# Six column pieces of W1 behind the first keys, and a key product over two heads of both batches, in a planned DeltaNet and MLP kernel

## Chip, cores and metric

One core of one Trainium2 chip runs the whole program. The metric is the device time of one execution in microseconds (us); lower is better. The kernel before was timed three times: median 530.33, lowest 530.28, highest 531.17.

## What is computed

Four batches, 8 heads, 768 positions, head size 48, all float32. First a delta-rule recurrence for each batch and head, then a normalised two-layer MLP with a residual over the 384 joined head outputs:

```
k_n = k / (norm(k, axis=-1) + 1e-6)
for t in range(S):
    y[t]  = q[t] @ state
    v_old = k_n[t] @ state
    state = state + beta[t] * outer(k_n[t], v[t] - v_old)
x  = y with its heads joined              # (4, 768, 384)
xn = (x - mean) / sqrt(var + 1e-6) * g_ln
out = x + relu(xn @ w_ch1) @ w_ch2        # 384 -> 1536 -> 384
```

## The kernel before

**Chunks.** The 768 positions are cut into 12 chunks of 64 (`C`), and a chunk into two blocks of 32 (`BK`). All 32 pairs of batch and head go through a chunk together: four groups of 8 heads by partition half and position in the row (`hp`, `e`, `g`). Inside a chunk the recurrence becomes matmuls: the products of keys with keys and of keys with queries, the inverse of a triangular matrix for each block, a correction step (`u`), the output (`y`) and the update of the state (`s_all`).

**Engines.** TensorE turns keys and queries (`first_kt`, L840, for early chunks) and does all products. The stages of `recur` are: keys times state (L1216 into `two`), corrections in three products (L1256: diagonal block, below, diagonal block), queries times state (L1216 into `by`), state update (L1281) and output (L1271). ScalarE copies a correction result out of PSUM at L1266 and the output of a chunk at L1312. VectorE subtracts at L1221 and L1262.

**The inverses.** Chunks 0 and 1 use `gram_near`, a 16-row elimination on VectorE (`rows_near`, L1088 and L1095) and a join of the two halves on TensorE (`near_join`, L1140). Later chunks take a 32-row elimination for two chunks at once (`rows_inverse`: L1157, 31 pairs of L1178 and L1185, and L1190, which writes the result). Its diagonal blocks come from copies on ScalarE: for chunks 2 and 3 L907 (with L911 for the block below the diagonal), behind the product `gram` (L896); from chunk 4 on L1030 and L1042.

**The merged key product.** From chunk 4 on `gram_queries` makes the key-key and key-query products of a chunk in one go, in two halves (`gram_half`, matmuls at L1017): half `g` writes the PSUM pair `two` (`g` = 0) or `by` (`g` = 1) for batch parity `g` and all four head pairs `j`. A matmul has 48 rows and 32 columns of stationary data and sits on one of eight tiles of the array. Where the block `b` equals `g` it streams 128 columns (`w` = `C`, two segments), otherwise 64 (`w` = `BK`). After it ScalarE copies the diagonal blocks (L1030, three copies of 128 elements per half) and the off-diagonal ones (L1042, two copies of 256), and VectorE masks the query product into `pt` (L1035).

**The MLP.** A chunk gives 256 rows. Chunks 0 to 2 run the first layer directly (L1561: twelve feature tiles `f0` to `f11`, three matmuls each, one for each 128 rows of W1), later chunks in a form with fewer products (`eleven`, L1492). The second layer is L1583 for chunk 0 and `seven` (L1664) afterwards, with combinations of weights and activations made on GpSimd and VectorE.

**Weights.** W1 and W2 arrive as 64-bit words on ScalarE's DMA queue, in 12 pieces of 768 KB (`fetch`), and are made into float32 by `convert`: two steps on ScalarE (L798, L806), one on VectorE (L803) and one on GpSimd (L816). A piece of W1 is 128 rows by 768 columns, 6 KB in one run per row, so the first feature tiles need three pieces. The three pieces with the first 768 columns are converted in two halves of 384 columns.

**Order.** The order of the instructions is worked out when the kernel is built. `Line.add` records each step with its engine, an assumed cost, what it reads and writes, and for MLP products a due time. `Line.schedule` places the steps by priority, and `emit` issues them in that order; every engine then works strictly in its own order. The lists `DUE`, `CAP`, `T0` and `OFF` shift due times, limits, earliest starts and priorities. `PASS`, `UPER` and the numbers in `pe(...)` are the costs that the planner assumes for short matmuls. `after=` in a step orders the plan alone; on the chip an instruction waits only for data that it reads or overwrites. Matmuls at L1745 keep TensorE busy in the first part and give nothing to the result.

**DMA queues.** SP issues keys, queries, values, most of beta and the outputs. ScalarE issues half of chunk 0's keys and all pieces of W1 and W2. GpSimd issues eight small loads of beta and the norm weights.

Of the kernel before, what the change touches and what calls it, by code (L numbers as in the profile page):

```python
# [56 lines left out]
def act(n):  # L57
    return 0.17 + 0.83e-3 * n
# [371 lines left out]
def kernel(  # L430
# [34 lines left out]
    UPER = 0.0076  # L465
# [57 lines left out]
    pmask = sb("pmask", [128, 2, C])  # L523
# [4 lines left out]
    lane = sb("lane", [128, 6])  # L528
    beta_s = sb("beta_s", [128, NEAR, FB])
# [24 lines left out]
    DUE = [-305.067857599, -184.157488926, 455.196580585, 43.3608971536, 325.931658715, 418.81557092, 734.822875439, 596.087521503, 954.313194593, 1226.15149798, 1753.77174886, 1187.43924725, -1.6924469742, 7.47712706956, 1.31274637377, 1177.34078649]  # L554
    CAP = [747.889715428, 1212.19696458, 1084.81830387, 1850.25080892, 1448.91733639, 908.561376039, 705.970562755, 575.226842462, 821.351411096, 750.46942201, 1687.9172189, 1227.4281115, 847.781737921, 881.489018474, 1102.45793961, 1447.53022967, 1091.57755388]
    T0 = [32.9830988769, 43.9377940451, 29.0921020937, 44.9281472705, 63.7206388166, 107.721780452, 109.01717894, 42.4201425188, 137.327678312, 9.9371017997, 7.55135349446, 21.1072922972, 47.3695615515, 3.2653345546, 12.003557196, 58.3820362978, 9.11313409582, 34.3183793157, 80.7294725245, 31.0940483985, 65.2240956281, 73.1210354066, 26.5270080195, 53.6799046277, 66.9289646085, 120.165225966]
# [39 lines left out]
    def dma(eng, out_, in_, n, ns, r=(), w=(), **kw):  # L596

        cost = 0.65 if eng == "Pool" else 0.39 if ns == 300 else 0.68 if ns in (16.5, 16) else 0.46 if ns == 168 else 0.62 if n < 128 else 0.53
        add(eng, cost, lambda: QUEUE[eng].dma_start(out=out_, in_=in_), r, w, bulk=n * ns / 16e3, pk=ns, **kw)  # L599
# [64 lines left out]
    for e in range(2):  # L664
        c_pool(
            lambda e=e: nc.gpsimd.affine_select(
                out=pmask[half(e), 0], in_=pmask[half(e), 0], compare_op=ALU.is_gt, fill=0.0, base=0,
                pattern=[[1, C]], channel_multiplier=-1,
            ),
            0.3, ["pmask"],  # L670
        )
    for x in range(4):
        c_pool(
            lambda x=x: nc.gpsimd.affine_select(
                out=pmask[quad(x), 1], in_=pmask[quad(x), 1], compare_op=ALU.is_gt, fill=0.0, base=BK * (x % 2 - 1),
                pattern=[[1, C]], channel_multiplier=-1,
            ),
            0.3, ["pmask1"], r=["pmask"],
        )
# [71 lines left out]

    def tb_keys(i, kind):

        if kind == "blk":
            return [("blk", i, hp, m, u) for hp in range(2) for m in range(2) for u in range(2)]
        return tb_nat(i, (kind,))

    def tb_nat(i, kinds=(0, 1)):
        return [("tb", i, e, g, *o) for g in kinds for e in range(2) for o in ((), (0,), (1,), (2,))] + [("tbpad", i)]


    pieces = [
        (w1_sb[:, t, f : f + WN], w_ch1.bitcast(U32)[t * 128 : (t + 1) * 128, 2 * f : 2 * (f + WN)], ("w1", t, f // WN))
        for f in range(0, DFF, WN)
        for t in range(KC)
    ] + [
        (
            w2_sb[:, t : t + 2],
            w_ch2.bitcast(U32)[t * 128 : (t + 2) * 128].rearrange("(t p) n -> p t n", p=128),
            ("w2", t // 2),  # L770
        )
        for t in range(0, FT, 2)
    ]
    BUF = [3, 4, 0, 1, 2, 5, 6, 0, 1, 2, 0, 1]

# [3 lines left out]
    def fetch(i, **kw):  # L779
        line.part += 1  # L780
        dst = words[BUF[i]].rearrange("p n w -> p (n w)")
        src = pieces[i][1]
        if len(src.shape) == 3:
            dst = dst.rearrange("p (t n) -> p t n", t=2)
        dma("ACT", dst, src, 128, 300, w=WORD_KEYS[BUF[i]], after=raw_keys(0) if i < 2 else (), **kw)

    def convert(i, c0=0, n=WN, **kw):
# [19 lines left out]
        if len(dst.shape) == 3:  # L807
            f0 = c0 // DM
            dst, keys = dst[:, f0 : f0 + n // DM], [key + (f0 + x, y) for x in range(n // DM) for y in range(2)]
            shape = lambda x: x.rearrange("p (t n) -> p t n", n=DM)  # L810
        else:
            dst, keys = dst[:, cols], [key + (c0 // 384 + x,) for x in range(n // 384)]
            shape = lambda x: x
# [183 lines left out]
    def gram_half(c, g, ps, pk, **kw):  # L997
# [5 lines left out]

        def segs(ap, step, n):
            return bass.AP(tensor=ap.tensor, offset=ap.offset, ap=[ap.ap[0], [step, 2], [1, n]])

        def prod():
            for j in range(NP):
                for hp, e in hp_e:
                    lk, lq = (((2 * x + g) * NP + j) * C for x in (key_half(c, hp, e), e))  # L1010
                    for b in range(2):
                        o = ps[quad(2 * (e ^ hp) + b), hp, j * 2 * C : (j + 1) * 2 * C]
                        if b == g:
# [878 lines left out]
```

## Time and profile before

| | us |
|---|---|
| median of 3 runs | 530.33 |
| the profiled execution | 531.07 |
| its span | 529.2 |
| TensorE matmul busy | 501.5 |
| VectorE busy | 369.4 |
| GpSimd busy | 211.3 |
| ScalarE busy | 196.7 |
| TensorE idle from 100 to 500 us | 5.0 |

The profile is of one execution. The time of that execution is 1.9 us longer than its span, which runs from the first to the last event that the profiler saw. A line of a timeline gives the start, the length, the engine, the source line and the operation; in brackets stands the idle time before it and what ended it. In the names of engines PE is TensorE's matmul, PEld its weight load, DVE VectorE, ACT ScalarE, POOL GpSimd and SP SyncE; a "q" behind a name is its instruction queue. A matmul of the source is two instructions in the trace, because float32 goes through in two passes, so a stage of 32 matmuls shows as x64. Where a trace misses records, a stage shows fewer.

### The profile page before, as it was taken

Reading aid. Unit: us, or ns where it says so; the run is one execution under the profiler, and the core shown is the slowest. Engines: PE = TensorE matmul, PEld = TensorE weight load, DVE = VectorE, ACT = ScalarE, POOL = GpSimd, SP = SyncE. Lnnn points to the kernel's source line nnn. Section 1 sums busy time; section 2 is a strip of 40 time slices with the busy share of each in tenths; the row PEclk is TensorE's granted clock in tenths of the full one; section 3 lists DMA queues with packets and bytes.
Section 4 is the critical chain, followed back from the end, with each engine's and each line's share of the span. In section 5 each row is a group of like instructions: output and inputs, shape, how many; then the busy total and the mean of one; then the engine's idle time right before and its main releaser. Section 6 shows DMA issues by size and latency. Waiting matters only on the chain.

```text
span 529.2 us, 22198 instructions
## 1 busy us (share of the span) xinstructions
PE 501.5 (95%) x9706; PEld 455.5 (86%) x9706; DVE 369.4 (70%) x849; ACT 196.7 (37%) x420; POOL 211.3 (40%) x320
## 2 busy tenths in 40 slices
PE   5967799999999999999999989999999999999996
PEld 3746677768898999989999879999889999999995
DVE  1899559997399866889895589895688893452331
ACT  2834875513812623525204522513523213242030
POOL 6151422236333560642724242452351815235352
PEclk8576779999999999999999999999999999999999
DMA  9965544365645445455311435221233010221101
GB/s 156 281 140 122 86 129 130 94 93 86 86 67 84 90 81 81 94 75 115 59 31 19 67 86 92 51 61 33 58 70 91 1 30 5 63 62 29 31 2 30
DMA packets 157457, 40.53 MB, mean 77 GB/s; under 512 B 150816, under 2 KB 153888, under 8 KB 157360
## 3 DMA queue, kind: packets, MB, share of 16 engines
q1 hardware_dynamic: 153520, 29.40, 31.4%
q10 hardware_dynamic: 3552, 9.63, 5.7%
q8 instruction: 76, 1.25, 1.0%
q0 software_dynamic: 288, 0.07, 0.1%
q14 instruction: 21, 0.17, 0.1%
HBM read 30.82 MB, written 8.26 MB: 74 GB/s over the span
## 4 chain that ended last, share of the span: by engine, by line
PE 86%; DVE 6%; issue 2%; DMA 2%; ACT 2%; SPq 1%; POOL 0%; DVEq 0%; ACTq 0%
PE f L1664 28%; PE f L1492 25%; PE f L1561 10%; PE two L1256 4%; PE f L1583 3%; PE by L1216 2%; PE two L1216 2%; PE by L1271 2%; PE two L1281 2%; PE two L1017 2%; DMA kr<-in_k_dram 1%; PE f L1140 1%; SPq L599 1%; DVE tmp L1088 1%; PE by L1017 1%
## 5 line engine op out<-in xcount | busy, mean ns | idle before, releaser
L1650 POOL TENSOR_TENSOR h_all<-h_all 128x256 f32<-128x256 f32 x99 | 73.9, 751 | 79.1 <-PE f L1664 65.9
L1664 PE MATMUL f<-w_sb,h_all 128*128 128x192 f32 x396 | 97.1, 333 | 1.4 <-ACT xln L1336 0.8
L1664 PE MATMUL f<-words,h_all 128*128 128x192 f32 x396 | 90.1, 329 | 0.0
L1492 PE MATMUL f<-xnt,w_sb 128*128 128x128 f32 x648 | 87.1, 277 | 0.4 <-issue 0.4
L1492 PEld LDWEIGHTS f<-xnt,w_sb 128*128 128x128 f32 x648 | 80.0, 192 | 1.6 <-ACT xnt L1377 0.9
L1664 PEld LDWEIGHTS f<-w_sb,h_all 128*128 128x128 f32 x396 | 66.3, 190 | 5.1 <-issue 2.3
L1515 DVE TENSOR_TENSOR h_all<-f,h_all 128x512 f32<-128x512 f32 (+1 forms) x90 | 49.5, 555 | 28.9 <-PE f L1492 19.8
L1664 PEld LDWEIGHTS f<-words,h_all 128*128 128x128 f32 x396 | 67.6, 190 | 1.1 <-ACT xln L1336 0.2
L1689 POOL TENSOR_TENSOR words<-h_all 128x128 f32<-128x128 f32 x66 | 32.8, 515 | 86.0 <-ACT h_all L1512 76.4
L1185 DVE TENSOR_TENSOR xb<-xb,tmp 128x31 f32<-128x31 f32 (+15 forms) x155 | 61.3, 396 | 4.0
L1178 DVE TENSOR_TENSOR tmp<-xb,gb 128x31 f32<-128x31 f32 (+15 forms) x155 | 60.0, 387 | 5.2 <-POOL xb L1164 1.0
L1561 PE MATMUL f<-xnt,w_sb 128*128 128x256 f32 x216 | 54.6, 399 | 1.2 <-issue 1.2
L1561 PEld LDWEIGHTS f<-xnt,w_sb 128*128 128x128 f32 x216 | 41.5, 198 | 8.2 <-issue 1.7
L1266 ACT COPY u<-two 128x768 f32<-128x768 f32 x24 | 19.2, 800 | 51.3 <-PE two L1256 43.8
L1492 PE MATMUL f<-second,w_sb 128*128 128x128 f32 x216 | 33.1, 276 | 1.7 <-POOL second L1472 1.7
L1512 ACT ACTIVATE h_all<-f 128x512 f32<-128x512 f32 (+1 forms) x36 | 17.4, 489 | 42.7 <-PE f L1492 31.0
L1682 DVE TENSOR_TENSOR o<-f,x 128x192 f32<-128x192 f32 x33 | 11.6, 352 | 30.5 <-PE f L1664 22.7
L1664 PE MATMUL f<-w_sb,words 128*128 128x192 f32 x132 | 32.1, 328 | 0.0
L1570 ACT ACTIVATE h_all<-f 128x256 f32<-128x256 f32 x36 | 13.7, 384 | 49.2 <-PE f L1561 49.0
L1492 PEld LDWEIGHTS f<-second,w_sb 128*128 128x128 f32 x216 | 29.2, 192 | 2.0 <-POOL second L1472 2.0
L1512 ACT ACTIVATE h_all<-h_all 128x512 f32<-128x512 f32 (+1 forms) x36 | 18.7, 521 | 29.4 <-DVE h_all L1515 29.3
L856 POOL TENSOR_TENSOR v<-v,knrms 128x768 f32<-128x768 f32 x10 | 15.3, 1533 | 30.4 <-PE f L1561 11.4
(194 smaller groups left out, 858.6 us busy)
## 6 DMA issues: line engine op xcount, KB each, us to landing
words<-in_moe_w_ch_dram ACTq DMA_DIRECT2D x8, 768.0 KB
out_dram<-o SPq DMA_DIRECT2D x48, 96.0 KB
xld<-xlt SPq DMA_DIRECT2D x9, 384.0 KB
xnt<-xld SPq DMA_DIRECT2D x36, 96.0 KB
tb<-in_q_dram SPq DMA_DIRECT2D x40, 64.0 KB
tb<-in_k_dram SPq DMA_DIRECT2D x32, 64.0 KB
v<-in_v_dram SPq DMA_DIRECT2D x8, 192.0 KB
w_sb<-in_moe_w_ch_dram ACTq DMA_DIRECT2D x2, 768.0 KB
```

Of the source, the lines that this page charges most:

```text
L1178: lambda j=j, n=n, w=w, t=t: nc.vector.tensor_tensor(out=t, in0=xb[:, 0:n, j : j + 1].to_broadcast([128, n, w]), in1=gb[:, j : j + 1, j + ...
L1185: "DVE", dve(n * w), lambda t=t, rest=rest: nc.vector.tensor_tensor(out=rest, in0=rest, in1=t, op=ALU.subtract),
L1216: nc.tensor.matmul(dst[half(e), hp, j], src[drows(hp), (e if n else key_half(c, hp, e)) * GP + j], s_all[drows(hp), e, j], start=(n == 0 o ...
L1256: nc.tensor.matmul(*args(e, e ^ hp, 2 * j + hp))
L1266: add("ACT", act(768), lambda: nc.scalar.copy(u_j, p_2), TWO, uk, after=["nought", *SMALL] if not c else (), **kw)
L1492: nc.tensor.matmul(wide(p[:, o : o + 128]), w[:, f : f + 128], r, start=start and m == n == 0, stop=stop, skip_group_check=True)
L1512: add("ACT", act(128 * m), lambda: nc.scalar.activation(to[0], p, ACTF.Relu), pk, to[1])
L1515: add("DVE", dve(128 * m), lambda v=ps(p): nc.vector.tensor_tensor(out=to[0], in0=v, in1=y[0], op=op), [*pk, *y[1]], to[1])
L1561: nc.tensor.matmul(p[:, 0:TOK], w1_sb[:, t, f * 128 : (f + 1) * 128], xnt[:, t], start=(t == 0), stop=(t == KC - 1))
L1650: add(eng, cost, lambda: e.tensor_tensor(out=out_, in0=x, in1=y, op=op), r, w, port=2 if eng == "Pool" else 1, pr=-2)
L1664: lambda f=f, t=start and f == 0: nc.tensor.matmul(p[:, 0:D2], lhs(f), rhs[:, f], start=t, stop=(f == F2 - 1), skip_group_check=True),
L1689: lambda f=f + i: e.tensor_tensor(out=s3[f], in0=one(0, 0)[0](f), in1=one(1, 0)[0](f), op=ALU.subtract),
```

## The change

The pieces of W1 are cut by columns: six pieces of 256 columns with all 384 rows, in runs of 2 KB. A piece carries two feature tiles. A small ScalarE copy that reads chunk 0's raw keys stands ahead of all fetches, and each piece is converted whole. The merged key product takes in each half two of the four head pairs, of both batch parities. The masks (`pmask`) and the copies behind the product follow, and the off-diagonal copy becomes four copies of 128 elements per half. The planner's costs for two kinds of short matmuls are changed, and the four lists have new numbers, so that all instructions are ordered anew. The numbers of the lists are left out here.

```diff
-    UPER = 0.0076
+    UPER = 0.0102
+    GPER = 0.0125
...
-    pmask = sb("pmask", [128, 2, C])
+    pmask = sb("pmask", [128, NP, C])
...
+    seen = sb("seen", [128, 2])
...
     pieces = [
-        (w1_sb[:, t, f : f + WN], w_ch1.bitcast(U32)[t * 128 : (t + 1) * 128, 2 * f : 2 * (f + WN)], ("w1", t, f // WN))
-        for f in range(0, DFF, WN)
-        for t in range(KC)
+        (
+            w1_sb[:, :, f : f + WN // KC], w_ch1.bitcast(U32)[:, 2 * f : 2 * (f + WN // KC)].rearrange("(t p) n -> p t n", p=128),
+            ("w1", f * KC // WN),
+        )
+        for f in range(0, DFF, WN // KC)
     ] + [
...
-        dma("ACT", dst, src, 128, 300, w=WORD_KEYS[BUF[i]], after=raw_keys(0) if i < 2 else (), **kw)
+        dma("ACT", dst, src, 128 * src.shape[1], 300 / src.shape[1], w=WORD_KEYS[BUF[i]], after=["seen"], **kw)
...
+        HP = NP // 2
+
         def prod():
-            for j in range(NP):
-                for hp, e in hp_e:
-                    lk, lq = (((2 * x + g) * NP + j) * C for x in (key_half(c, hp, e), e))
-                    for b in range(2):
-                        o = ps[quad(2 * (e ^ hp) + b), hp, j * 2 * C : (j + 1) * 2 * C]
-                        if b == g:
+            for j in range(HP):
+                for r in range(2):
+                    for hp, e in hp_e:
+                        lk, lq = (((2 * x + r) * NP + HP * j + g) * C for x in (key_half(c, hp, e), e))
+                        for b in range(2):
+                            at = (r * HP + j) * 2 * C
+                            o = ps[quad(2 * (e ^ hp) + b), hp, at : at + 2 * C]
+                            if b == r:
...
         for e in range(2):
-            o, w = jn(goff[quad(2 * e + g), i])[:, :, hs], v[quad(2 * e + g), :, :, BK * (1 - g) : BK * (2 - g)]
-            add("ACT", act(256), lambda o=o, w=w: nc.scalar.copy(o, w), pk, [("go", i, e, x, g) for x in range(2)], **kw)
+            for r in range(2):
+                o = mine(jn(goff[quad(2 * e + r), i]))[:, :, HP * r : HP * r + HP]
+                w = v[quad(2 * e + r), :, HP * r : HP * r + HP, BK * (1 - r) : BK * (2 - r)]
+                add("ACT", act(128), lambda o=o, w=w: nc.scalar.copy(o, w), pk, [("go", i, e, x, r) for x in range(2)], **kw)
...
+    add(
+        "ACT", 0.2, lambda: nc.scalar.copy(seen, kraws[0].rearrange("p (h d) -> p h d", d=DP)[:, 0:2, 0]),
+        [x for x in raw_keys(0) if x[0] == "kr"], ["seen"], pr=-100,
+    )
...
-    for c0 in (0, 384):
-        for i in range(3):
-            convert(i, c0, 384, pr=-50 if c0 == 0 else -10)
+    for i in range(3):
+        convert(i, pr=-50)
+    line.part += 3
```

How the built instructions move, around the start (lines of the kernel before): TensorE turns the keys of chunk 1 ahead of the first key product (L923); the products of chunks 2 and 3 (L896) stand ahead of chunk 1's join (L1140), with the first feature tile of the MLP between them; behind the first correction product of chunk 2 stand nine more matmuls of the first MLP's second layer (L1583) than before. On ScalarE two fetches stand behind the copy into `seen` and five more some twenty instructions later; four conversions stand ahead of the first copy at L1266. On VectorE the subtraction at L1262 of chunk 0 stands ahead of chunk 1's elimination. Instead of 13 fillers (L1745) there are 17.

## The prediction

> **What bounds the kernel now.** I read the first page first: which engine is full, and when.
>
> ```profile
> span 529.2 us, 22198 instructions
> PE 501.5 (95%) x9706; PEld 455.5 (86%) x9706; DVE 369.4 (70%) x849; ACT 196.7 (37%) x420; POOL 211.3 (40%) x320
> ...
> PE   5967799999999999999999989999999999999996
> ...
> PEclk8576779999999999999999999999999999999999
> ```
>
> TensorE is the full engine, except in the first five or six slices of 13.2 us, where it also runs at a lower granted clock. The view by stretches gives sizes (second column: length; then busy time of PE, PEld, DVE, ACT, POOL, granted clock, DMA share, GB/s).
>
> ```profile
> 0.00:65.00 65.00, 48.33 (x1239) 38.36 (x1239) 45.35 (x141) 34.50 (x62) 26.43 (x43) 0.69 0.77 159
> 65.00:100.00 35.00, 33.80 (x664) 26.34 (x665) 26.52 (x59) 21.69 (x40) 8.64 (x6) 0.88 0.46 128
> 100.00:250.00 150.00, 149.58 (x3149) 132.86 (x3148) 119.78 (x254) 57.59 (x140) 61.67 (x84) 1.00 0.51 85
> 250.00:400.00 150.00, 145.43 (x3048) 137.08 (x3047) 113.96 (x260) 51.12 (x115) 63.30 (x100) 1.00 0.29 57
> 400.00:500.00 100.00, 100.00 (x1439) 97.27 (x1438) 56.57 (x122) 27.29 (x58) 40.63 (x69) 1.00 0.14 37
> ```
>
> From 100 to 500 us TensorE idles 5.0 us of 400. There only removed TensorE work helps. Before 65 us the granted clock is 0.69 and the work is a serial chain. The chain of waits shows its head and where the MLP of chunk 0 joins (start, length, what):
>
> ```profile
> 1.65 7.50 DMA kr<-in_k_dram
> ...
> 9.39 1.95 PE by L840 x8
> ...
> 12.01 2.02 PE two L923 x64
> ...
> 64.96 1.15 PE f L1561 x2
> 66.11 1.20 issue
> ```
>
> The first keys are on the way until 9.15 us; the MLP starts at 64.96. The third view is the timeline, for what releases chunk 2, the first chunk with a 32-row inverse:
>
> ```profile
> 65.91 4.10 ACT L907 COPY gdiag<-two 32x512 f32<-32x512 f32 x4
> 70.05 1.25 DVE L1157 STREAM_TRANSPOSE gb<-gdiag 128x1024 f32<-128x1024 f32 x1 [4.32 <-ACT gdiag L907]
> 112.95 2.11 DVE L1190 STREAM_TRANSPOSE xt<-xb 128x1024 f32<-128x1024 f32 x1
> ```
>
> VectorE waits for ScalarE's diagonal copies (L907, begun at 60.25), works on the inverse almost without a gap and ends at 115.06; TensorE's first correction product of chunk 2 (L1256) starts at 115.23. So **115.23 is set by VectorE**, and from there to the last matmul (510.66 + 13.71 = 524.37) TensorE is full: 409.1 us. The chain L907, inverse, chunk 2 is what an earlier start must shorten.
>
> **The merged key product.** Its own time, where no record is missing:
>
> ```profile
> 372.42 1.14 PE L1017 MATMUL two<-kq 48*32 48x128 f32 x64
> 373.30 1.16 PE L1017 MATMUL by<-kq 48*32 48x128 f32 x64
> 374.38 0.59 PE L1664 MATMUL f<-w_sb,h_all 128*128 128x192 f32 x2
> ```
>
> From start to start: 0.88 and 1.08 us, the second with the change to large matmuls. A half uses eight array tiles. With g fixed, four of them get only 128-column matmuls and four only 64-column ones. Dense rows give 0.84 ns per column (L1561: 1.29 us for six of 256). A wide tile thus needs 4 heads x 2 passes x 128 x 0.84 = 0.86 us, the measured 0.88: the wide tiles bound the half. After, each tile gets two of each: 2 x 2 x (128 + 64) x 0.84 = 0.65. Lower bounds from other rows of 64 short matmuls: L1256 0.73 (32x32 tiles), L1281 0.89, L1216 1.08. So a half saves between 0 and 0.23; I take 0.2, since 32-column tiles are nearest to L1256. Sixteen halves, all in the full stretch (130 to 375): **3.2 us, bounds 0 to 3.7**.
>
> A rule speaks against this: the Trainium skill, "TensorE: Matmul & The Clock Gate", The HAM clock gate (Wait — 56ns, not 53.3ns?), says that matmul starts never come closer than about 25 ns. By it a half would be 64 x 25 = 1.6 us in either order and save nothing. The trace disagrees: 0.88 us for 64 is 13.8 ns.
>
> The off-diagonal copies (L1042) double in number, 32 to 64, at 128 elements. The 256-element form takes 0.37; the 128-element copy from the same bank (L1030) 0.38, half of 0.37 is 0.19; I take 0.3. ScalarE gets 7.4 us more (bounds 0.2 to 12.5), 0.46 per half. It is 37% busy, so the cover is TensorE's MLP work before the next user of the bank (L1216): at least 12 x 0.325 = 3.9 us behind a pair in the new order. The first bank needs 3 x 0.38 + 4 x 0.3 = 2.3 us, and its copies can start 0.8 us before the pair ends. So nothing; without the cover 0.46 to 0.76 per half.
>
> **W1 in six pieces.** Same bytes; packets of 2 KB instead of 6 KB. The 3 KB packets of W2 land as fast as 6 KB ones (issue at 34.11: 347 GB/s at 36 to 38 us; issue at 71.33, 6 KB: 329 and 268 at 72 to 76), so nothing is charged. Conversions become 12 of 768 columns for 9 of 768 and 6 of 384: three full ScalarE pairs (0.91 and 0.90) for six half pairs (0.55 twice), 1.2 us less; VectorE about 0.5 less, GpSimd 1 less (6 x 0.9 against 3 x 1.47), all beside other work. The larger mask adds at most 1.9 us on GpSimd before 11 us, under its idle until 14.2.
>
> **The fetches wait for the keys** (the copy into "seen"). Behind it on ScalarE stand two fetches and the key copies, which need the same keys anyway: 0.2 us. What goes: a W1 fetch issued at 2.33, which shared the DMA engines with the keys (4 to 8 us: 280 GB/s, of which the keys are 0.39 MB in all). The keys alone, at 153520 packets for 31.4% of 16 engines' span (17.3 ns each), are 2048 x 17.3/16 = 2.2 us. They are issued by 2.4 us, and a 96 KB load that nothing disturbs lands 2.5 us after its issue (xnt<-xld at 310.12): with part of the 2.2, about 5.6 instead of 9.15 (estimate). But in the new order TensorE turns the keys of chunks 0 and 1 before the first product, and chunk 1's four loads follow on SP (issued by 6.68 in this trace): 7.5 to 9.5. The first product ends at 10.5 to 13 instead of 14.03. I take 2.5 us earlier.
>
> The Trainium skill, "DMA: Bandwidth & Descriptors", Queues, rings and completion order, says that each DMA engine takes turns between the queues packet by packet. By that the short key packets fell behind the 6 KB ones; the 9.15 agrees.
>
> **The order anew**, up to chunk 2. (a) ScalarE: five fetches now stand together at some 22 to 25 us, and four conversion pairs (1.8 each) stand ahead of the first copy of chunk 0's corrections (L1266, at 38.77 before); they need landed pieces. VectorE: the subtraction L1262 now stands ahead of chunk 1's 16-row elimination; before, it ran at 41.84 with its product done at 41.1. I take 3.5 us earlier for the copy of chunk 0's output (47.57), bounds 0 and 5. (b) TensorE: the products of chunks 2 and 3 (L896) now stand ahead of chunk 1's join (L1140); before, that join and 2.15 us of issue stood in front. From output copy to the first L907: 12.7 us before (47.57 to 60.25). Without the wait for the first L896 half (1.5), the join's half (1.3) and the issue gap (2.15), but with three conversion steps (0.9 each) between, partly in waits that were there, 8.5 to 10. The first L907 thus starts at 44.1 + 8.8 = 52.9. (c) From there to chunk 2's inverse: 54.8 before. The first diagonal transposes follow the copies the same way; VectorE has three conversions fewer there (5 to 2, 0.56 each) and no wait of 1.15 for the product of queries, but the join's predicated copy (0.73) more: 52.8. Chunk 2 starts at 105.7. TensorE gets there in time: between the third feature tile and that product it has 35.9 us, and it reaches that tile when L907 and L911 (11.2 us together) and the join are done, about 66. (d) Counting instructions behind that product in both orders: equal but for nine second-layer matmuls of the first MLP (L1583, 0.65 each), 5.9 us more, and the cheaper halves, 3.2 less: +2.7. MLP and recurrence stand as far apart as before (from the output product of chunk 6 to its MLP 20.8 us of TensorE work, 18.1 before, where 1.67 was idle), so I keep the 5.0 us of idle.
>
> **Sum:** 105.7 - 115.2 + 5.9 - 3.2 = **-6.8 us**. The profiled execution took 531.07 (span 529.2 and 1.9 around it): 524.3. Against the median of 530.33, 0.74 lower: 523.5.
>
> **Rivals.**
> 1. The start is given back: the five fetches share DMA with keys and values at the 172 to 250 GB/s of 20 to 26 us, 3.9 MB take 16 to 23 us, and ScalarE stands before a conversion with the correction copies behind it. For: in this trace a conversion waited 2.69 us (h_all at 30.27). Against: one piece alone lands 3.7 us after its issue. Chunk 2 then starts at about 110: -5.2 + 5.9 - 3.2 = -2.5: 527.8. Chance 0.16.
> 2. Slower: the first bank of the key product is held longer by the copies, and L1216 waits in all 16 halves, 0.76 each, 12.2 us, because ScalarE's ReLUs (0.4 to 0.5) stand between them. -6.8 + 12.2 = +5.4: 535.7; it turns from 0.43 per half. Against: L1216 waited 0.5 us in all for L1030. Chance 0.09.
> 3. The product gains nothing, as where 64 short matmuls take 0.89 or more: -3.6: 526.7. Chance 0.12. The skill's rule of 25 ns would end here too.
> 4. The new order also loses the 5.0 us of idle at 250 to 400: 518.5. Chance 0.10.
> 5. The change does not act: fetches are not what delays the keys and the order is no denser; only the halves and the nine matmuls: 530.33 + 2.7 with chunk 2 unmoved, 533. Chance 0.02.
>
> The forecast (519.5 to 526.5) has 0.51.
>
> **How the numbers follow.** Range 517.0 to 529.3: it takes in the forecast, 1, 3 and most of 4; outside lie 2, 5 and tails, 0.17. About 0.2% (1.06 us) is what a measurement of this kernel can tell from no change: faster 0.85 (forecast, 3, 4, most of 1), same 0.04 (the rest of 1), slower 0.11 (2 and 5).
>
> **What would show it.** First transposes before 7 us; first product ending before 13; the first diagonal copy near 53; the first correction product of chunk 2 near 106, released by VectorE; a half of the merged product at 0.65 to 0.8; idle of 250 to 400 near 5. Wrong if ScalarE shows waits for W1 or W2 pieces of several us before chunk 0's corrections, or if L1216 is released by the off-diagonal copies.

## The result, and the profile after

The changed kernel took **537.99 us** in the median of 20 runs, the kernel before 530.56 beside it: ratio **1.0115** (95% interval 1.009 to 1.0141). It is slower by some 6 us; 523.5 was forecast. Its profiled execution took 538.39 us, 7.3 more than that of before (531.07). Ratios compare means without the executions that were unusually long for their kernel (three of the twenty here, which is why 1.0115 is below the ratio of the medians), and of the one trace of such an execution, that of `after_light`, only the first 70 us are used.

The page of the changed kernel's profile, the lines that answer to those of before:

```profile
span 536.3 us, 22217 instructions
PE 504.7 (94%) x9714; PEld 455.9 (85%) x9714; DVE 373.8 (70%) x846; ACT 198.4 (37%) x447; POOL 212.1 (40%) x317
...
PE   6768789999999899999999999899999999999996
...
PEclk9675979999999999999999999899999999999999
```

Two things are to be seen: the clock digits start well (9 and 6 for 8 and 5) and then fall to 5 in the fourth slice, and there is an 8 late in the clock row (slice 26, about 343 us) that the old kernel does not have. The same stretches as before:

```profile
0.00:65.00 65.00, 49.17 (x1126) 37.59 (x1127) 43.74 (x139) 38.04 (x61) 26.86 (x40) 0.74 0.74 167
65.00:100.00 35.00, 31.61 (x785) 25.14 (x783) 27.81 (x62) 16.48 (x34) 7.48 (x5) 0.90 0.49 102
100.00:250.00 150.00, 145.63 (x2987) 127.14 (x2987) 113.47 (x240) 55.42 (x147) 63.44 (x85) 1.00 0.49 81
250.00:400.00 150.00, 147.28 (x3119) 139.69 (x3117) 118.56 (x256) 54.66 (x137) 60.53 (x98) 0.99 0.31 62
400.00:500.00 100.00, 99.55 (x1476) 95.33 (x1476) 60.85 (x133) 28.84 (x61) 41.37 (x69) 1.00 0.15 38
```

From 100 to 250 us TensorE is busy 145.63 us, where it had been busy 149.58. A stretch that was almost full now has holes.

**Where the time went**, from the two traces (the kernel before, the changed one, the difference):

| | before | after | |
|---|---|---|---|
| first key product ends | 14.03 | 11.10 | -2.9 |
| first correction result copied (L1266, L1279) | 38.77 | 40.77 | +2.0 |
| output of chunk 0 copied (L1312, L1325) | 47.57 | 49.02 | +1.5 |
| first diagonal copy (L907, L913) | 60.25 | 58.70 | -1.6 |
| first correction product of chunk 2 | 115.23 | 112.21 | -3.0 |
| from there to the end of the last matmul | 409.1 | 419.3 | +10.2 |

The 10.2 are: nine more second-layer matmuls (6.7 by their rows, 113.02 to 122.44), 1.9 more idle time (6.9 against 5.0), 1.7 for one clock window of 3.4 us at half speed at 343 us, 1.0 less in the sixteen halves of the key product, and 0.9 that no row accounts for. The earlier start of chunk 2 is no gain by itself. The nine matmuls stood ahead of it before, so their move alone is worth more than the 3.0 us, and ahead of chunk 2 TensorE is now idle for 19.8 us, 17.9 before.

**The early hole.** TensorE in the first join of the changed kernel:

```profile
27.25 1.29 PE L1153 MATMUL f<-pt,second 32*32 32x32 f32 x128 [0.37 <-DVE pt L1148]
...
29.61 1.07 PE L1153 MATMUL f<-xt,pt 32*32 32x32 f32 x102
34.71 0.63 PE L1153 MATMUL f<-xt,pt 32*32 32x32 f32 x26 [4.03 <-issue]
35.27 2.08 PE L1765 MATMUL f<-u 128*128 128x256 f32 x4
37.28 1.50 PE L1269 MATMUL two<-v,xt 32*32 32x48 f32 x64
```

The join begins at 27.25, 3.1 us earlier than before (30.37). In the middle of one and the same product TensorE then stands still for 4.03 us, and the profile names nothing it waits for ("issue"). The first correction product starts at 37.28; it was 37.22 before. The whole gain is gone, and the product takes 1.50 us instead of 0.88: the clock record says half speed from 32.4 to 56.3 us without a break.

What it waits for can be counted. The page lists a DMA queue that carries instructions; the trace has its 76 packets, each of 16 KB:

```profile
q8 instruction: 76, 1.25, 1.0%
```

TensorE's weight loads and matmuls together are 19,428 instructions, 256 for each packet. Counted in the order of the trace, with TensorE's 80 others (semaphores above all), the four longest "issue" stops of both traces (before: 56.60 and 66.11 us; after: 30.68 and 62.34) fall at instruction 1986, 2498, 962 and 2242, each two behind a multiple of 256 less 64, and each ends 1.3 to 1.4 us after such a packet has landed. So a stop stands where one block of 256 instructions ends and the next has not come. At 30.68 the next block's packet had not started; it started at 32.20 and landed at 33.29. The block before it had been begun at 28.16, and all of it was started within 2.3 us, because it is mostly short matmuls (the first product of the join above, 128 matmul instructions and as many weight loads, took 1.29 us); its successor's packet started 4.05 us after it was begun. In the kernel before, the same distance, from the begin of a block to the start of the next one's packet, is 0.8 us in the median of the run and 1.0 to 2.7 us in the first 45 us; in the changed kernel it is 2.5 to 4.0 us there. The Trainium skill, "Runtime: NRT & Kernel Launch", Instruction fetch mechanics, says that instructions come in 16 KiB blocks of 256, each fetched while the one before is executed; the packets agree. It calls the crossing mostly hidden; here it cost 4.03 us, and the measurement decides.

Why the packet is late shows in the DMA columns, 25 to 50 us, of the kernel before and of the changed one:

```profile
25.00:50.00 25.00, 17.84 (x597) 13.81 (x595) 23.07 (x70) 9.96 (x19) 8.31 (x8) 0.70 0.57 125
```

```profile
25.00:50.00 25.00, 18.64 (x556) 14.09 (x558) 17.48 (x44) 13.16 (x19) 11.35 (x9) 0.64 0.78 210
```

The weight pieces that no longer run beside the first keys run here: 210 GB/s for 125, the DMA engines busy 78% for 57%. ScalarE's queue, which carries them, moves 160 GB/s of the 210, and 58 of the 125 before.

**The hole in the full stretch.** At 185 us TensorE stops for 2.44 us. SP, ScalarE and TensorE there:

```profile
175.91 0.54 SPq L601 DMA_DIRECT2D xld<-xlt  x1
176.50 0.52 SPq L601 DMA_DIRECT2D out_dram<-o  x1
177.11 0.66 SPq L601 DMA_DIRECT2D kr<-in_k_dram  x1
177.86 1.21 SPq L601 DMA_DIRECT2D out_dram<-o  x2
179.16 2.06 SPq L601 DMA_DIRECT2D kr<-in_k_dram  x3
181.32 2.64 SPq L601 DMA_DIRECT2D xnt<-xld  x4
```

```profile
186.15 1.30 ACT L1390 ACTIVATE xnt<-xnt,g_sb 128x256 f32<-128x256 f32 x3 [3.87 <-DMA xnt<-xld]
187.37 0.63 ACT L1586 ACTIVATE h_all<-f 128x256 f32<-128x256 f32 x2
...
187.87 0.56 PE L1680 MATMUL f<-words,h_all 128*128 128x192 f32 x2 [2.44 <-ACT h_all L1586]
```

Read from below: TensorE waits for a ReLU, the ReLU stands in ScalarE's queue behind L1390, L1390 waits for the four loads of the MLP input, and SP issues these behind eight other DMAs. From 99 to 191 us SP starts 148 DMAs, never more than 2.7 us apart and mostly 0.5 to 0.7 us.

In the kernel before the same loads went out later still, at 186.59, and ScalarE waited longer for them than now:

```profile
191.15 1.31 ACT L1377 ACTIVATE xnt<-xnt,g_sb 128x256 f32<-128x256 f32 x3 [5.92 <-DMA xnt<-xld]
```

That wait cost TensorE nothing, because the last ReLU of the running MLP (L1570) stood ahead of it and had run at 178.28. The new order puts two ReLUs behind the wait. So the hole needs both, loads that go out late and ReLUs that stand behind their arrival. The stop at 340 us has the same form: L1390 waits 7.26 us for its loads, and TensorE 2.23 us for a ReLU behind it.

### The profile page after: what moved, and what is told of

It is laid out like the page before. It is cut to its first block, busy times and chain, and to the rows that moved or that the text cites. A ratio compares the mean times of both kernels' runs of the same rounds, so it can differ in the third digit from the quotient of the medians.

```text
span 536.3 us, 22217 instructions
## 1 busy us (share of the span) xinstructions
PE 504.7 (94%) x9714; PEld 455.9 (85%) x9714; DVE 373.8 (70%) x846; ACT 198.4 (37%) x447; POOL 212.1 (40%) x317
## 4 chain that ended last, share of the span: by engine, by line
PE 79%; DVE 6%; DMA 6%; ACT 4%; SPq 2%; issue 2%; POOL 1%; ACTq 0%; DVEq 0%
PE f L1680 27%; PE f L1508 23%; PE f L1577 8%; PE two L1269 5%; DMA words<-in_moe_w_ch_dram 3%; SPq L601 2%; PE f L1599 2%; PE by L1229 2%; PE two L1229 2%; DMA xnt<-xld 2%; ACT gdiag L913 2%; PE two L1027 1%; PE by L1284 1%; PE two L1294 1%; PE by L1027 1%
## 5 line engine op out<-in xcount | busy, mean ns | idle before, releaser
L1680 PE MATMUL f<-w_sb,h_all 128*128 128x192 f32 x396 | 96.7, 333 | 0.2 <-DVE tmp L1191 0.2
L1666 POOL TENSOR_TENSOR h_all<-h_all 128x256 f32<-128x256 f32 x99 | 75.7, 771 | 52.9 <-PE f L1680 45.7
L1680 PE MATMUL f<-words,h_all 128*128 128x192 f32 x396 | 91.2, 333 | 4.7 <-ACT h_all L1586 2.4
L1508 PE MATMUL f<-xnt,w_sb 128*128 128x128 f32 x648 | 89.4, 278 | 0.2 <-DVE words L1698 0.2
L1680 PEld LDWEIGHTS f<-words,h_all 128*128 128x128 f32 x396 | 67.9, 192 | 6.2 <-POOL second L1488 2.7
L1680 PEld LDWEIGHTS f<-w_sb,h_all 128*128 128x128 f32 x396 | 67.3, 191 | 2.5 <-DVE tmp L1191 0.5
L1191 DVE TENSOR_TENSOR tmp<-xb,gb 128x31 f32<-128x31 f32 (+15 forms) x155 | 64.6, 417 | 4.5
L1198 DVE TENSOR_TENSOR xb<-xb,tmp 128x31 f32<-128x31 f32 (+15 forms) x155 | 63.4, 409 | 3.9
L1279 ACT COPY u<-two 128x768 f32<-128x768 f32 x24 | 19.1, 797 | 61.6 <-PE two L1269 45.5
L1680 PE MATMUL f<-w_sb,words 128*128 128x192 f32 x132 | 32.2, 329 | 0.3 <-DVE o L1698 0.3
L862 POOL TENSOR_TENSOR v<-v,knrms 128x768 f32<-128x768 f32 x10 | 15.3, 1528 | 36.1 <-DMA v<-in_v_dram 24.3
L1525 ACT COPY h_all<-f 128x512 f32<-128x512 f32 (+1 forms) x18 | 8.6, 480 | 52.4 <-PE f L1508 41.3
```

Of the source, the lines that this page charges most:

```text
L1191: lambda j=j, n=n, w=w, t=t: nc.vector.tensor_tensor(out=t, in0=xb[:, 0:n, j : j + 1].to_broadcast([128, n, w]), in1=gb[:, j : j + 1, j + ...
L1198: "DVE", dve(n * w), lambda t=t, rest=rest: nc.vector.tensor_tensor(out=rest, in0=rest, in1=t, op=ALU.subtract),
L1279: add("ACT", act(768), lambda: nc.scalar.copy(u_j, p_2), TWO, uk, after=["nought", *SMALL] if not c else (), **kw)
L1508: nc.tensor.matmul(wide(p[:, o : o + 128]), w[:, f : f + 128], r, start=start and m == n == 0, stop=stop, skip_group_check=True)
L1666: add(eng, cost, lambda: e.tensor_tensor(out=out_, in0=x, in1=y, op=op), r, w, port=2 if eng == "Pool" else 1, pr=-2)
L1680: lambda f=f, t=start and f == 0: nc.tensor.matmul(p[:, 0:D2], lhs(f), rhs[:, f], start=t, stop=(f == F2 - 1), skip_group_check=True),
```

## The experiments

Theory A: the loss is made in the first 70 us, by weight pieces that delay TensorE's instruction blocks. Theory B: it is made later, where TensorE waits at 185 and 340 us; made sharper as S: SP's queue sets these waits however early the engines are. Theory C: only the order, with more work behind chunk 2. Each ratio is to the kernel before on the same chip, with its 95% interval.

**The same kernel again** (`after_again`, no edit).

> The changed kernel once more, unaltered, for a second trace and a time on the same chip as the runs beside it. Theory A (the loss is made in the first 70 us: TensorE stands still for its next block of instructions at 30.7 us while the W1 pieces travel, and its clock then halves): the wait of about 4 us in the first join and the low clock behind it come again, ratio about 1.0115. Theory B (the loss is made later, where TensorE waits at 185 and 340 us for ScalarE, which waits for a DMA): those two waits, 2.4 and 2.2 us, come again at the same instructions. Theory C (neither; the order simply leaves more TensorE work behind chunk 2's first correction product): both differ from trace to trace, and the time stays at 1.0115.

Measured: 1.0135 (1.0098 to 1.0172), 536.98 us. Both holes come again: 2.7 us of "issue" in the first join, with the packet again at 32.20, the correction result copied at 40.78, chunk 2 at 111.72; 2.8 us at the same L1680 at 185, here with a window of half clock behind it (188.3 to 191.7). The wait at 340 us did not come again; in the trace of `after_ident` it did (2.2 us). So A and B both describe something that belongs to the order, and only the wait at 340 comes and goes.

**Fewer weight bytes** (`after_light`; control `before_light`).

```diff
+        if 2 <= i <= 6:
+            dst, few = dst[:, 0], src[:, 0]
```

and in the kernel before, whose pieces have another shape:

```diff
+        if 2 <= i <= 6:
+            dst, few = (dst[:, 0], src[:, 0]) if len(src.shape) == 3 else (dst[:, 0:512], src[:, 0:512])
```

> The changed kernel with two thirds of the bytes of the third to seventh piece of W1 and W2 left out (only the first 128 rows of a W1 piece and half of a W2 piece are fetched, the rest is zero), all instructions in the same order, two short VectorE fills added in its idle time. Theory A: the block of instructions that TensorE lacks at 30.7 us starts about 1 us after the one before is begun instead of 4, the wait falls from 4.0 us to 1.5 or less, the clock is not halved behind it, the first correction result is copied at 38 instead of 40.8, and the time falls by 3 to 6 us against the changed kernel, to 532 to 535. Theory B: the first 70 us may gain, the waits at 185 and 340 stay, and the time falls by less than 1.5 us. Theory C: no fall beyond 1 us.

> The kernel before with two thirds of the bytes of the third to seventh weight piece left out (zeros in their place), the control to the same edit in the changed kernel, which took 0.8% off its ratio. Theory A (in the new order these pieces travel while TensorE needs its next blocks of instructions, in the old one less so): it gains less than half of that, ratio 0.996 to 1.000. Rival: the pieces disturb both orders alike, ratio 0.990 to 0.994, and they are no part of the difference.

The bytes left out are zeros in both kernels, so only their times mean anything. Measured: 1.0039 (1.0008 to 1.0071) and 0.998 (0.9961 to 0.9999). The bytes cost the changed order 0.8 to 1.0% by the ratios, 0.6% by the medians on the same chip (536.98 to 533.53 us), and the old one 0.2%: theory A. In the trace the late packet starts 2.07 us after the block ahead of it is begun instead of 4.05, and the stop shrinks from 4.0 to 2.1 us, not to the expected 1.5; the copy comes at 39.53, not at 38. Over all traces that distance is 3.8 to 4.4 us in the seven of the changed order with full pieces, 2.1 and 2.6 in the two with light ones, and 0.8 to 1.6 in the five of the old order. The length of the stop varies more (2.7 to 4.0 us with full pieces and nothing in the hole, 2.1 and 2.9 with light ones). Other DMAs (keys, queries) are in that stretch too, so the weight pieces are about half of the delay, not all of it.

**Fillers in the hole** (`after_gap`).

```diff
+            if c == 0:
+                for _ in range(10):
+                    nc.tensor.matmul(f_[0][:, 256:512], ident, ident[:, 0:1].to_broadcast([128, 256]))
             prod(pz_, es, xt)
```

> The changed kernel with ten more filler matmuls of 256 columns (some 4 us of TensorE at full clock) ahead of the second product of chunk 0's join, where TensorE otherwise stands still; they read the identity. Theory A: the join ends at the same time, since the block of instructions lands no earlier, but the clock stays at 1.0 behind it; the first correction product and its copy come 1 to 2 us earlier, the output of chunk 0 about 3 us earlier, the time falls by 2 to 4 us. Rival to it: the halved clock costs nothing because other waits hide it, or the 40 more instructions push the block's edge so that the join ends later: no change or 1 to 2 us slower.

Measured: 1.0124 (1.0088 to 1.016). The mechanism held and the time did not follow. The granted clock stays at 1.0 from 30.7 to 51.2 us. The first product of corrections takes 0.88 us for 1.50, the output of chunk 0 is copied at 45.67 for 49.03, chunk 2 starts at 109.77 for 111.72. Behind it 418.5 us follow instead of 416.6: the stop at 183 is still there (2.3, behind a GpSimd step that waits for the same loads), and merged halves and MLP products stand at "issue" for 0.5 to 1.2 us where they did not before. Ten matmuls are 40 instructions, and every later block edge, the place where one block of 256 ends, has moved by them.

**Fillers that read another tile** (`after_ident`).

```diff
-        nc.tensor.matmul(f_[0][:, 256:512], nought, nought[:, 0:1].to_broadcast([128, 256]))
+        nc.tensor.matmul(f_[0][:, 256:512], ident, ident[:, 0:1].to_broadcast([128, 256]))
```

> The changed kernel with its fillers reading the identity instead of the first 128 columns of the tile that takes the correction results. Theory A': the copy of the first correction result, which starts at 40.77 when the fillers behind the product have ended at 40.68, then starts about 39.0, right after the product (38.78); chunk 0's output 1 to 1.8 us earlier, the time 1 to 2 us lower. Rival: the copy gains but the gain is lost before 70 us to the wait of chunk 1, time within 0.5 us of the changed kernel.

Measured: 1.0112 (1.007 to 1.0154), no change. The filler's input is the first 128 columns of `u`, which the correction copy overwrites; without that the copy starts 0.1 us behind the product (39.59) instead of 2.0. But the output of chunk 0 is copied at 48.35 (49.02), the first diagonal block at 58.42 (58.70), and chunk 2 starts at 112.01. The rival holds: the 1.2 us are almost lost again by 60 us.

**The MLP input's DMAs on ScalarE's queue** (`after_act`; control `before_act`).

```diff
-            dma("SP", xld, xlt, 128, 168, [("xlt", g) for g in range(2)], ["xld"], **kw)
+            dma("SP", xld, xlt, 128, 168, [("xlt", g) for g in range(2)], ["xld"], via="ACT", **kw)
...
-                    [("xnj", c % 2, j)], after=xk, **kw,
+                    [("xnj", c % 2, j)], after=xk, via="ACT", **kw,
```

> The changed kernel with the store and the four loads that turn the MLP input (xld<-xlt, xnt<-xld) issued on ScalarE's queue instead of SP's, every engine's order otherwise kept. Theory S (SP's queue, which issues without a pause from 111 to 191 us, is late by 4 us more than the engines and sets when the first such loads are issued, 181.1 to 182.9 us in five traces however early the engines were): the loads go out some 4 us earlier, the wait of TensorE at 183 to 185 us (2.3 to 4.5 us in five traces) shrinks below 1, and the time falls by 2 to 4.5 us against the changed kernel, to a ratio of about 1.005 to 1.009. Rival: the transfers, not their issue, are late, or ScalarE standing at the issue holds its ReLUs back: the wait stays or moves, the ratio stays at 1.011 to 1.0135.

> The same edit in the kernel before, where no wait stands at that place. Theory S: within 0.2% of the kernel before, since its SP queue had pauses and the loads were there in time; ScalarE's issues cost nothing that TensorE sees. Rival: if the five issues on ScalarE hold its ReLUs, it is slower by 1 us or more, and the same loss hides in the other run.

Measured: 1.0043 (1.0021 to 1.0065) and 0.9972 (0.9948 to 0.9996). Theory S: the same transfers, issued elsewhere, take 0.7 to 0.9% off. The longest ReLU wait of TensorE behind 100 us is now

```profile
PE f L1577 <- ACT h_all L1586: 1.1, 1, 1.1
```

No run shows what it would gain to move only the two ReLUs ahead of L1390. The control was expected to stay the same and gained 0.28%: SP's queue cost the old order a little too (2.5 us idle behind chunk 2 instead of 5.0). The Trainium skill, "DMA: Bandwidth & Descriptors", Rules for kernel authors, says that spreading DMAs over issuing engines brings no bandwidth and only saves issue time; that agrees, since issue time was what was short here.

**Three edits together** (`after_fix`: the ten fillers, the identity, ScalarE's queue).

> The changed kernel with three edits together: the ten fillers ahead of the second product of the first join, all fillers reading the identity, and the MLP input's DMAs on ScalarE's queue. If what the start gains was taken back by SP's queue, the sum is more than its parts: 5 to 8 us below the changed kernel, ratio 0.998 to 1.003. If the parts are independent: 3 to 5 us, ratio 1.003 to 1.007. If later waits take back everything: 1.01.

Measured: 1.0074 (1.0039 to 1.0109), at the slow edge of "independent" and above ScalarE's queue alone. Against the trace of ScalarE's queue alone the start gained 3.9 us (chunk 2 at 109.85 for 113.74, which is late: three other traces without fillers in the hole have 111.7 to 112.2), and 417.5 us follow for 414.0. That made the moved block edges the suspect, and the next run tests it.

**The same without added instructions** (`after_refill`: ScalarE's queue, the identity, and four of the planned fillers moved and widened).

```diff
+    for s in line.fills:
+        if 27.8 < s.start < 36.5:
+            s.start, s.fn = 29.05, wide        # 512 columns
```

> The changed kernel with the MLP input's DMAs on ScalarE's queue, fillers that read the identity, and the four fillers that stand around the second product of the first join moved ahead of it and made 512 columns wide, so that TensorE works while its block of instructions is on the way, with no instruction added (ten added matmuls shifted every later block edge, and merged products then stood 0.7 to 1.2 us at an edge). Theory A: the clock is at 1.0 from about 32 to 43 us, the start gains 2 to 4 us on the run with ScalarE's queue alone, and later edges stay where they were: ratio 0.997 to 1.001. Rival: what the start gains is given back later whatever the edges do (the transfers of keys and values, not SP's queue, limit 110 to 190 us): ratio 1.003 to 1.007.

Measured: **0.9983** (0.9959 to 1.0007), 0.9% less than with ten added matmuls and 0.6% less than ScalarE's queue alone. The first join now:

```profile
27.90 1.29 PE L1153 MATMUL f<-pt,second 32*32 32x32 f32 x128 [1.37 <-DVE pt L1148]
...
29.64 3.61 PE L1880 MATMUL f<-ident 128*128 128x512 f32 x8
33.19 1.02 PE L1153 MATMUL f<-xt,pt 32*32 32x32 f32 x96
35.55 0.45 PE L1153 MATMUL f<-xt,pt 32*32 32x32 f32 x32 [1.35 <-issue]
36.98 0.88 PE L1269 MATMUL two<-v,xt 32*32 32x48 f32 x64 [0.97 <-POOL tb L1793]
```

The wide fillers work through the time in which the block is on its way; 1.35 us of the stop are left; the product of corrections runs at full clock. Chunk 2 starts at 108.84, 6.4 us before the old kernel (in four traces of the old start it begins at 113.8 to 115.2), and behind it all waits of TensorE are

```profile
PE two L1269 <- issue: 0.6, 1, 0.6
PE f L1599 <- POOL w_sb L822: 0.6, 1, 0.6
PE f L1508 <- DVE words L1698: 0.2, 1, 0.2
```

Behind chunk 2 411.1 us follow, 6.4 less than with ten added matmuls. Of the 6.4, 3.2 are "issue" stops (0.6 us in all for 3.8) and 1.9 are waits for a ReLU, so moved block edges are shown for about half of it. The planned order, rid of both holes, is about as fast as the old one, and theory C is not borne out. It is not faster either: the 5.0 to 6.4 us won ahead of chunk 2 only pay for the nine matmuls (6.7) behind it.

**Both losses at once** (`after_light_act`: the light weight pieces and ScalarE's queue).

> The changed kernel with both: the weight bytes left out, and the MLP input's DMAs on ScalarE's queue. If the two losses (the first 70 us, and SP's queue at 185 us) are separate, the gains add: 1.0115 to 1.0135 less 0.008 less 0.008, ratio 0.994 to 0.998. If one loss hides the other, the ratio is 1.002 to 1.004, as with each alone.

Measured: 0.9976 (0.9952 to 1.0). The gains add; the two holes are separate. ScalarE's queue is no full cure, though: in this trace ScalarE's own issue of three loads takes 4.08 us from 176.61, and TensorE waits 2.2 us for the ReLU behind it, with a window of half clock after that (181.2 to 184.6).

**The merged product alone** (`before_halves`: the new split with its masks and copies in the kernel before, order kept).

```diff
-            for j in range(NP):
-                for hp, e in hp_e:
-                    lk, lq = (((2 * x + g) * NP + j) * C for x in (key_half(c, hp, e), e))
...
+            for j in range(HP):
+                for r in range(2):
+                    for hp, e in hp_e:
+                        lk, lq = (((2 * x + r) * NP + HP * j + g) * C for x in (key_half(c, hp, e), e))
```

> The kernel before with the new merged key product alone (two heads of both batches per half, the masks and copies that go with it), planned order unchanged. The forecast's size: 0.2 us a half, 3.2 us in all, ratio 0.994. What the trace of the changed kernel shows (0.82 from start to start instead of 0.875): 0.06 a half, 0.9 us in all, ratio 0.998 to 0.999. Rival: the off-diagonal copies, 32 more on ScalarE, hold the PSUM banks and so the next products: ratio above 1.002.

Measured: 0.9999 (0.9976 to 1.0022). The forecast's 0.994 is excluded, no loss by the copies is seen, and 0.06 us a half is within the interval. A pair of halves in the changed kernel:

```profile
170.06 0.96 PE L1027 MATMUL two<-kq 48*32 48x128 f32 x54
170.75 0.29 PE L1027 MATMUL by<-kq 48*32 48x128 f32 x1
170.76 0.38 PE L1027 MATMUL two<-kq 48*32 48x64 f32 x9
170.87 0.27 PE L1027 MATMUL by<-kq 48*32 48x128 f32 x2
170.88 0.22 PE L1027 MATMUL two<-kq 48*32 48x64 f32 x1
170.88 1.09 PE L1027 MATMUL by<-kq 48*32 48x128 f32 x61
171.90 0.59 PE L1680 MATMUL f<-w_sb,h_all 128*128 128x192 f32 x2
```

From start to start: 0.82 (170.06 to 170.88) and 1.02, where the old order took 0.88 and 1.08.

**Sets of short matmuls** (`after_more`, `after_sets`: 64 further matmul instructions ahead of some halves, overwritten by them). `narrow(w)` is the half with `w` columns in every matmul, `old` the half of the kernel before, `real` the new half in a given order.

```diff
+            if c == 9:
+                narrow()
+            if c == 10:
+                old()
+            if c == 11:
+                narrow(C)
             prod()
```

```diff
+            if c == 7:
+                narrow(96)
+            if c == 9:
+                real([(j, r, hp, e, b) for r in range(2) for j in range(HP) for hp, e in hp_e for b in range(2)])
+            if c == 10:
+                real([(j, r, hp, e, b) for j in range(HP) for hp, e in hp_e for b in range(2) for r in range(2)])
+            if c == 11:
+                real([(j, r ^ b, hp, e, b) for j in range(HP) for r in range(2) for hp, e in hp_e for b in range(2)])
             prod()
```

> The changed kernel with four sets of 64 short matmuls added ahead of the real halves, each overwritten by them: chunk 9's halves after the same number of matmuls with 32 columns each, chunk 10's after the old order (one batch parity), chunk 11's after 64 columns each. If columns bound a half: 32 columns 0.43 us, old order 0.87, 64 columns 0.43 to 0.5, real half 0.82. If the rate of matmuls bounds it: all at 0.7 to 0.8, however few the columns, and the new split had no more than 0.06 to gain.

> The changed kernel with a further set of 64 short matmuls ahead of some real halves, each overwritten by them. Open is why a half of the new split takes 0.82 us when its columns alone take 0.65 by dense rows. Theory Q (matmuls start in order, so one that waits for its busy array tile holds those behind it; in the new order wide and narrow ones alternate within each group of eight tiles): chunk 7's set with 96 columns everywhere, the same sum, takes 0.65 to 0.7; chunk 11's set, the real matmuls with each group of eight all wide or all narrow, 0.65 to 0.7; chunk 10's, both matmuls of a tile one behind the other, 1.2 or more; chunk 9's, parity outermost, 0.82 as now. Rival R (a floor per matmul or per change of width, whatever the order): 0.78 or more in chunk 7, 0.8 or more in chunk 11, and about 0.82 in chunk 10.

Measured, from the first start to the last of the 64, us, in sets that nothing interrupts (one or two of each kind):

| set | us |
|---|---|
| 32 columns each | 0.56, 0.66 |
| 64 columns each | 0.64 |
| 96 columns each | 0.75 |
| the new order (real half) | 0.82 |
| real, each group of eight all wide or all narrow | 0.83 |
| the old order | 0.87 |
| real, parity outermost | 0.89 |
| real, both matmuls of a tile in a row | 1.01 |

Neither theory fits. Sets of 32 and of 64 columns take almost the same, 9 to 10 ns from start to start, and order matters (0.82 to 1.01 for the same matmuls), but the waiting theory wanted 0.65 to 0.7 for groups of equal width and got 0.83, and the floor theory wanted 0.78 for 96 columns and got 0.75. What sets 0.82 stays open; the size that the forecast lacked is measured.

**The parts that stood by themselves** (`before_act_halves`: the kernel before with ScalarE's queue and the new split).

> The kernel before with the two edits that gained or did no harm by themselves: the MLP input's store and loads on ScalarE's queue, and the new split of the merged key product. Additive: 0.9972 and 0.9999 give 0.997; by the trace's 0.06 us a half 0.996. If the new order of the changed kernel were needed for a gain, it is 1.000.

Measured: **0.9948** (0.9921 to 0.9974), 528.14 us: faster than both kernels. The new order of all instructions is not needed for it. The better part of the gain is ScalarE's queue; whether the split adds to it is not shown (ScalarE's queue alone gave 0.9972, and the intervals overlap).

## Why the prediction was wrong, by its own steps

- **The keys: right.** The first transposes stood at 6.19 (forecast before 7), the first key product ended at 11.10 (10.5 to 13). In part this was luck: the product took 1.16 us for 2.02, because the clock was granted in full until 15.3 us (until 8.2 before), and the forecast had no such term.
- **Step (a), "I take 3.5 us earlier for the copy of chunk 0's output": this failed.** It came 1.5 us later. The join's first product was 3.1 us early, as the step needs; the second stood 4.0 us for a block of instructions, and from 32.4 us the clock was halved for 23.9 us; the step had put the wait for instructions and the clock at nothing. The forecast had the sign of it in hand: 2.15 and 1.2 us of "issue" in the old trace. It took them for gaps that a new order closes, and never asked what an "issue" of 2 us is. With the hole filled (`after_refill`) the copy came at 47.02, 0.6 us early, and chunk 2 6.4 us early; the 3.5 was too much even then.
- **Steps (b) and (c): nearly right.** From output copy to first L913 9.7 us (8.8 taken), from there to chunk 2's first correction product 53.5 (52.8). VectorE's part held (the inverse ended at 111.25, 52.6 after the first L913), but that VectorE would release the product did not: TensorE came to it at 112.21 without having been idle just before. "TensorE gets there in time" was wrong by 1.0 us.
- **Step (d), nine matmuls: right, a little small**, 6.7 for 5.9.
- **The halves: 0.06 us each for 0.2**, 1.0 in all for 3.2. The bounds (0 to 0.23) held; the value was taken at the wrong end. That 32-column tiles reach 0.73 for 64 matmuls of one width said nothing on two widths mixed.
- **The copies: right.** 0.26 to 0.29 us each (0.3 taken), hidden, and L1229 waited 0.1 us in all.
- **"I keep the 5.0 us of idle": failed.** It was the question of what is late next, and the answer was the loads on SP's queue and what stands behind them. The forecast compared distances on TensorE, where nothing was tighter, and counted neither SP's issues between the store and the loads of the MLP input nor what stands behind the wait for them on ScalarE, where the new order has two ReLUs that TensorE needs. 1.9 us of idle and 1.7 of half clock came of it; the runs with ScalarE's queue put the loss at 0.7 to 0.9% in the ratio.
- **The rivals.** The first had the direction (the start is given back) with another mechanism: ScalarE did stand 4.19 us ahead of the conversion of a weight piece at 24.93 (the profile names a key load as what ended it), one of the forecast's own signs of being wrong, but no step of the corrections was late by it: the next one, L1156, waited 1.94 us for TensorE. The second did not happen. The third was right on the product. The slower outcome had 0.11, on a mechanism that played no part.

Sum of the miss, in us: chunk 2's start 6.5, halves 2.2, idle 1.9, clock 1.7, nine matmuls 0.8, not accounted for 0.9, and 0.1 behind the last matmul and outside the span; together 14.1, which is 538.39 less 524.3. Taking out both holes does not make the forecast right: `after_refill` is 0.2% below the old kernel, where 1.3% was forecast. In its trace (526.82 us, where the median is 528.70) 2.5 us of the miss are left: chunk 2 starts 3.1 us later than forecast, the halves lack 2.2, the nine matmuls 0.8, and against that TensorE idles 3.8 us less than the forecast kept. Why the start gains no more stays open.

## What to carry to other kernels

Behind the first 15 us of these traces, every "issue" of more than a microsecond on TensorE was a block of instructions on its way: count 256 instructions per block, and ask of each moved burst of short matmuls how long a block lasts in it and what the DMA engines carry at that moment. Follow the queue that feeds the next stage (here SP's), not only the engine that is full, and look at what stands behind each wait for a load on its own engine: the same late loads cost nothing in the old order and 2.4 us in the new one. Adding instructions to a tuned stream moves every block edge behind them; widening instructions that are there does not.

## What the runs showed of the hardware that was not expected

- TensorE's instruction blocks share the DMA engines with data: the packet started 4.05 us after the block ahead of it was begun with five weight pieces under way, 2.07 with a third of their bytes, about 1 us in the median of the run.
- Behind a stop of 4.0 us in a stream of short matmuls the granted clock was half for 23.9 us, behind one of 2.7 us for 20.5 us (`after_again`); with ten fillers in the same place it stayed full until 51.2 us, with 3.6 us of wide fillers until 38.6 us.
- In the changed order the same DMAs cost 0.7 to 0.9% more of the whole time on SP's full queue than on ScalarE's, with the same bytes; in the old order 0.3%.
- 64 matmuls of 32 columns take 0.56 us, 8.9 ns from start to start, and the same 64 matmuls of mixed width 0.82 to 1.01 by their order.
